# Six V transfers on GpSimd's DMA queue, and the fourth head's K issued in earlier slots, at the start of an attention and MLP kernel

## The chip, the cores and the metric

One core of one Trainium2 chip. The metric is the device time of the whole kernel in microseconds (us), from one launch; lower is better. Engines are named as the profile names them: PE (TensorE, matmuls), PEld (its weight loads), DVE (VectorE), ACT (ScalarE), POOL (GpSimd) and SP (SyncE, which here only issues DMAs).

## The reference

```python
x  = A_x                                # 1 x 2048 x 512, bf16
xn = _layernorm(x)
s  = _A_ref(xn, k_cache, v_cache, wq, wo)   # 32 heads of 128, 2048 queries, 2048 keys:
                                            # softmax(q k^T / sqrt(128)) v, then @ wo
g  = _silu(_B_ref(xn, w1, w2, w3, w4))      # a mixer with shifted channels, then an MLP
return x + s * g
```

K and V come from a cache in HBM (32 heads x 2048 x 128 each). Nearly all the work is the attention: for each head, 2048 x 2048 scores, their exponentials, and the product with V.

## The kernel before, in words

**Units and slots.** The 32 heads are taken in 8 groups of four. A unit is one head with 512 of the 2048 queries; inside a group the four heads follow each other for the first 512 queries, then for the next, so units 0 to 3 are heads 0 to 3 with the first 512 queries. A unit has 8 slots, and the main loop (line 809) runs over all slots n; unit u has slots 8u to 8u + 7. Each slot does one `s_slot` (L196): two score matmuls of 128 keys each into PSUM, and one exponential over both on ACT (L207). Five slots later (at this place of the program) the matching `pv_slot` (L225) multiplies the exponentials with two blocks of V. So the scores of unit u begin in slot 8u, and its product with V in slot 8u + 5. A quarter of K (512 keys) serves two slots: slot 8u needs the first quarter of its head's K, 8u + 2 the second, 8u + 4 the third and 8u + 6 the fourth. A half of V serves four slots of the product.

**The order.** Every instruction is pinned to the program's order on its engine (`pin`), so each engine and each DMA queue runs its list in exactly the order in which the Python code makes it; an instruction whose data isn't there holds up all behind it on its engine. Small pieces of work are hung on slots with `at(n, ...)` and are made at the end of slot n.

**What else runs in the first slots.** Tokens are normalized tile by tile: `ln1_load` fetches a tile of x on GpSimd's queue, `ln1_stats` takes the mean and variance on DVE and the inverse root on POOL (`rsqrt`, L126 and L127), `ln1_apply` normalizes on DVE (L423) and `ln1_turn` transposes by DMA on SP's queue (L439) into `xnT`. The query projection of later units (`q_mm`) reads `xnT`; that of unit 4 stands in slots 22 and 23 and is the first that needs token tiles 4 to 7. For the first four units the sums of the exponentials are made by a matmul with ones (`sums`, L235), inverted on DVE (L245, tile `rc`), written to DRAM on SP's queue (L247, `dr`), read back spread over all partitions on the same queue (L277, `rb`), and `norm` (L280, L294) multiplies the product with V by it on DVE. Unit u has its `dr` in slot 8u + 11, its `rb` in slot 8u + 12 and its `norm` in slot 8u + 18. The product lies in one of two PSUM tiles (`psO`), so that the product of unit u + 2, from slot 8u + 21 on, waits for the `norm` of unit u.

**The loads that the change touches.** `load_k` (L153) fetches a quarter of one head's K with a transposing DMA (L158); `load_v` (L162) fetches half of one head's V (L168). Both are issued on SP's queue. Before the loop (lines 740 to 756) all of head 0 and 1, and the first two quarters of head 2's K, are issued; the rest of heads 2 and 3 hang on slots 2 to 22 (lines 766 to 768). Later groups (lines 773 to 782) load in the same way from SP's queue, hung on their own slots; the change leaves them as they are. Each DMA also waits, before it is issued, until the eighth one ahead of it in its kind of queue has landed, since the DMAs share eight semaphores in turn.

Of the kernel before, what the change touches and what calls it, by code (L numbers as in the profile page):

```python
# [17 lines left out]
def kernel(  # L18
# [15 lines left out]
    nc = tc.nc  # L34
# [28 lines left out]
    pin = tc.keep_in_program_order  # L63
# [78 lines left out]
    def at(n, fn):  # L142
        todo[n].append(fn)
# [9 lines left out]
    def load_k(h, pieces):  # L153
        w = Sk // KSPLIT
        for i in pieces:
            if i == 0:
                kTs[h] = kp.tile([P, Sk], BF16, name="kT")
            pin(nc.sync.dma_start(  # L158
                out=kTs[h][:, i * w:(i + 1) * w],
                in_=A_k_cache[0, h, i * w:(i + 1) * w, :], transpose=True))  # L160

    def load_v(h, halves):  # L162
        v = A_v_cache[0, h].rearrange("(i p j) d -> p i j d", p=P, j=KJ)
        for i in halves:
            if i == 0:
                vBs[h] = vp.tile([P, KC, Dh], BF16, name="vb")
            ks = slice(i * KSPLIT // 2, (i + 1) * KSPLIT // 2)
            pin(nc.sync.dma_start(  # L168
                out=vBs[h].rearrange("p (i j) d -> p i j d", j=KJ)[:, ks], in_=v[:, ks]))

    def load_w(h, eng=nc.sync):
# [266 lines left out]
    def ln1_turn(t):  # L438
        pin(nc.sync.dma_start_transpose(out=xnT[:, :, t * P:(t + 1) * P], in_=xns.pop(t)[:]))  # L439
# [304 lines left out]
    for h in range(HG - 1):  # L744
        load_w(h, nc.gpsimd)
    load_k(0, range(KSPLIT))
    load_v(0, (0, 1))
    load_k(1, range(KSPLIT))
    warm_up(WARM)
    mean_3 = first_stats()  # L750
    load_w(HG - 1, nc.gpsimd)
    for t in range(4, 8):
        ln1_load(t, nc.gpsimd)
    first_tokens()
    load_v(1, (0, 1))
    load_k(2, (0, 1))
    tokens = ((2, 4, 5), (5, 9, 11), (8, 12, 13), (11, 14, 14),
              (21, 27, 27), (26, 31, 31), (34, 37, 37), (38, 41, 41),
              (39, 45, 45), (47, 53, 53), (55, 61, 61), (63, 69, 69))
    for t, (stats, apply, turn) in enumerate(tokens, 4):  # L760
# [2 lines left out]
        at(stats, lambda t=t: ln1_stats(t))  # L763
        at(apply, lambda t=t: ln1_apply(t))
        at(turn, lambda t=t: ln1_turn(t))
    for n, load, h, piece in ((2, load_k, 2, 2), (4, load_k, 2, 3), (7, load_v, 2, 0), (15, load_k, 3, 0), (15, load_v, 2, 1),
                              (19, load_k, 3, 1), (20, load_k, 3, 2), (20, load_v, 3, 0), (21, load_k, 3, 3), (22, load_v, 3, 1)):
        at(n, lambda load=load, h=h, piece=piece: load(h, (piece,)))
    at(28, ph1_load)
    at(64, w2_load)  # L770
    for h in range(HG):
# [1 line left out]
    for g in range(NG - 1):  # L773
        b = (g * QT + QT - 1) * HG
        for hh in range(HG):
            h = (g + 1) * HG + hh
# [163 lines left out]
    halves = [psX.tile([P, D], FP32, tag="xm", name="ps_wo"), psO.tile([P, D], FP32, tag="ps_o", name="ps_wo")]  # L940
# [51 lines left out]
```

## Time and profile before

| | |
|---|---|
| Time, median of 3 runs | 1250.77 us (1249.69 to 1251.74) |
| Profiled execution: span from its first to its last instruction | 1248.0 us |
| Profiled execution: time of its own | not shown beside its span; the median of the runs is 2.8 us above the span |
| PE busy | 1240.0 us (99%) |
| ACT busy | 1128.1 us (90%) |
| DVE busy | 1115.1 us (89%) |
| POOL busy | 134.8 us (11%) |
| DMA, mean over the span | 104 GB/s |

How to read it: busy times are sums over the span, and PE's are modelled, since matmuls are pipelined. A view of the timeline has, in each row, the start (us from the span's start), the duration, the engine, the line of the kernel, the operation, and the tiles written and read; in brackets stands how long the engine was idle before it and which instruction ended that. This is inferred from semaphores: where the engine named had long been done, it was another, often a DMA. An engine with a "q" (SPq) is the issuing of a DMA, not the transfer; from issue to landing has rows of its own. Tile names are the program's: `kT` and `vb` are K and V of a head, `pT` the exponentials, `ps_s` and `ps_o` the scores and the product with V in PSUM, `xin` a tile of x, `acc` the running sum of exponentials.

### The profile page before, as it was taken

How to read it: one execution, taken by the hardware profiler on the slowest of the kernel's cores; microseconds unless marked ns; L12 is line 12 of the kernel's file. 1: busy time of each engine (PE TensorE's matmuls, PEld its weight loads, DVE VectorE, ACT ScalarE, POOL GpSimd, SP SyncE). 2: the span in 40 equal slices, each digit the busy share in tenths (PEclk: the TensorE clock that was granted, in tenths of full speed). 3: DMA queues.
4: the chain of work that ended last, by engine and by line, in shares of the span. 5: the costliest groups of instructions: out<-in, count | busy, mean ns of one | idle time of the engine just before them, and what ended most of it. 6: DMA issues, size and time to landing. Idle time of an engine off the chain costs nothing.

```text
span 1248.0 us, 16489 instructions
## 1 busy us (share of the span) xinstructions
PE 1240.0 (99%) x5808; PEld 597.1 (48%) x5808; DVE 1115.1 (89%) x1518; ACT 1128.1 (90%) x1285; POOL 134.8 (11%) x237
## 2 busy tenths in 40 slices
PE   9999999999999999999999999999999999999998
PEld 5444444444444444444444444444444444444444
DVE  7899999999899988889998889999888999888997
ACT  8999999888999888899998889998888999988992
POOL 4310003332101000000100000010000000000110
PEclk9999999999999999999999999999999999999999
DMA  9654353565624456243563345734345243653453
GB/s 183 138 115 73 72 135 73 124 134 111 153 63 112 104 103 118 51 94 73 108 155 85 68 77 106 135 81 81 82 103 121 55 89 68 125 140 75 106 156 99
DMA packets 240468, 129.32 MB, mean 104 GB/s; under 512 B 191296, under 2 KB 217280, under 8 KB 240384
## 3 DMA queue, kind: packets, MB, share of 16 engines
q1 hardware_dynamic: 231136, 102.89, 41.0%
q0 software_dynamic: 8672, 24.91, 7.5%
q8 instruction: 45, 0.74, 0.3%
q10 hardware_dynamic: 576, 0.46, 0.1%
q14 instruction: 39, 0.32, 0.1%
HBM read 83.62 MB, written 8.13 MB: 74 GB/s over the span
## 4 chain that ended last, share of the span: by engine, by line
PE 98%; ACT 1%; DVE 0%; issue 0%; POOL 0%; POOLq 0%
PE ps_s L122 36%; PE ps_o L122 35%; PE ps_m L122 10%; PE ps_q L122 9%; PE ps_wo L122 8%; ACT pT L207 1%; DVE acc L218 0%; ACT sq L513 0%; ACT pre L540 0%; DVE xnT L469 0%; DVE qT L193 0%; ACT xnT L471 0%; PE ps_sum L122 0%; DVE gf L350 0%; DVE xf L355 0%
## 5 line engine op out<-in xcount | busy, mean ns | idle before, releaser
L207 ACT ACTIVATE pT<-ps_s 128x1024 bf16<-128x1024 f32 x1024 | 1022.1, 1028 | 92.3 <-PE ps_s L122 77.4
L122 PE MATMUL ps_s<-qT,kT 128*128 128x512 bf16 x2048 | 608.8, 379 | 1.3 <-ACT pT L207 0.9
L122 PE MATMUL ps_o<-pT,vb 128*128 128x512 bf16 x2048 | 607.5, 379 | 0.0
L122 PEld LDWEIGHTS <-kT 128*128 128x128 bf16 x2048 | 231.6, 113 | 228.4 <-issue 4.5
L218 DVE TENSOR_TENSOR acc<-acc,pT 128x2048 bf16<-128x2048 bf16 x256 | 308.9, 1207 | 8.9 <-ACT pT L207 8.4
L122 PEld LDWEIGHTS <-vb 128*128 128x128 bf16 x2048 | 200.2, 98 | 225.6
L213 DVE TENSOR_TENSOR acc<-pT 128x2048 bf16<-128x2048 bf16 x128 | 156.3, 1221 | 32.8 <-ACT pT L207 32.4
L122 PE MATMUL ps_q<-xnT,wq_h 128*128 128x512 bf16 (+1 forms) x524 | 152.8, 374 | 0.6 <-ACT xnT L471 0.4
L122 PE MATMUL ps_wo<-wo_h,oT 128*128 128x512 bf16 (+1 forms) x460 | 135.3, 377 | 0.5 <-DVE qT L193 0.5
L287 DVE TENSOR_TENSOR oT<-ps_o,rb 128x512 bf16<-128x512 f32 x122 | 130.7, 1072 | 4.4 <-DMA rb<-dr 4.1
L373 DVE TENSOR_TENSOR s_acc<-ps_wo,s_acc 128x512 f32<-128x512 f32 x96 | 66.0, 688 | 42.7 <-PE ps_wo L122 42.6
L222 DVE TENSOR_TENSOR acc<-acc 128x1024 bf16<-128x1024 bf16 x128 | 87.5, 684 | 0.9
L260 DVE TENSOR_REDUCE sm<-accT 128x4 f32<-128x512 bf16 x122 | 83.1, 681 | 1.5 <-DMA accT<-acc 1.4
L193 DVE CAST qT<-ps_q 128x512 bf16<-128x512 f32 x109 | 75.0, 688 | 8.4 <-PE ps_q L122 7.7
L122 PEld LDWEIGHTS <-wq_h 128*128 128x128 bf16 x524 | 50.8, 98 | 60.8 <-issue 1.0
L122 PE MATMUL ps_m<-xn2T,w_sb 128*128 128x512 bf16 x224 | 77.1, 379 | 0.0
L122 PE MATMUL ps_m<-w_sb,h2T 128*128 128x512 bf16 x224 | 77.1, 379 | 0.0
L122 PEld LDWEIGHTS <-oT 128*128 128x128 bf16 x468 | 45.7, 98 | 55.2 <-issue 0.8
L671 POOL DMA_DIRECT2D w_sb<-in_B_w_dram x28 | 21.1, 754 | 370.6 <-PE ps_m L122 370.6
L223 DVE TENSOR_TENSOR acc<-acc 128x512 bf16<-128x512 bf16 x128 | 54.4, 425 | 4.4
L699 POOL DMA_DIRECT2D g_d<-xr x16 | 8.7, 546 | 438.0 <-DVE xr L697 372.2
L508 DVE SCALAR_TENSOR_TENSOR sq<-sq,pre 128x1024 bf16<-128x1024 bf16 x36 | 44.0, 1222 | 4.6 <-ACT sq L504 4.6
(87 smaller groups left out, 591.0 us busy)
## 6 DMA issues: line engine op xcount, KB each, us to landing
rb<-dr SPq DMA_DIRECT2D x127, 256.0 KB, 4.0
vb<-in_A_v_cache_dram SPq DMA_DIRECT2D x64, 256.0 KB, 3.3
w_sb<-in_B_w_dram POOLq DMA_DIRECT2D x28, 256.0 KB, 3.6
wo_h<-in_A_wo_dram SPq DMA_DIRECT2D x32, 128.0 KB, 2.9
wq_h<-in_A_wq_dram SPq DMA_DIRECT2D x28, 128.0 KB, 2.9
kT<-in_A_k_cache_dram SPq DMA_TRANSPOSE x128, 3.4
dr<-rc SPq DMA_DIRECT2D x128, 2.0 KB, 1.7
xr<-in_A_x_dram POOLq DMA_DIRECT2D x16, 128.0 KB, 2.4
```

The lines of the kernel that those rows point to most:

```text
L122: pin(nc.tensor.matmul(out=out, lhsT=lhsT, rhs=rhs, start=start, stop=stop))
L193: pin(nc.vector.tensor_copy(out=qT[:], in_=st[u].pop("psq")[:]))
L207: pin(nc.scalar.activation(out=s["pT"][-1][:, jj:jj + 2, :], in_=sps[:], func=ACT.Exp, scale=SCALE))
L213: pin(nc.vector.tensor_tensor(out=s["acc"][:], in0=s["pT"][0][:], in1=s["pT"][1][:], op=ALU.add))
L218: pin(nc.vector.tensor_tensor(out=a[:], in0=a[:], in1=st[u]["pT"][i][:], op=ALU.add))
L222: pin(nc.vector.tensor_tensor(out=a[:, 0:2, :], in0=a[:, 0:2, :], in1=a[:, 2:4, :], op=ALU.add))
L223: pin(nc.vector.tensor_tensor(out=a[:, 0, :], in0=a[:, 0, :], in1=a[:, 1, :], op=ALU.add))
L260: pin(nc.vector.tensor_reduce(out=sm[:], in_=s.pop("at")[:], axis=mybir.AxisListType.X, op=ALU.add))
L287: pin(nc.vector.tensor_tensor(out=oTs[(g, qt)][:, hh, :].rearrange(f, j=4), in0=s["o"].rearrange(f, j=4), in1=s["rb"].rearrange("x (p j) - ...
L373: pin(nc.vector.tensor_tensor(out=sa, in0=ps[:], in1=sa, op=ALU.add))
L508: pin(nc.vector.scalar_tensor_tensor(out=sq[:].rearrange(f2), in0=sq[:].rearrange(f2), scalar=1.0, in1=pre[:].rearrange(f2), op0=ALU.add, ...
L671: pin(nc.gpsimd.dma_start(out=w[:], in_=w3_v[:, :, fc * P:(fc + 2) * P]))
```

## The change

```diff
-    def load_v(h, halves):
+    def load_v(h, halves, eng=nc.sync):
...
-            pin(nc.sync.dma_start(
+            pin(eng.dma_start(
                 out=vBs[h].rearrange("p (i j) d -> p i j d", j=KJ)[:, ks], in_=v[:, ks]))
...
-    load_v(1, (0, 1))
+    load_v(1, (0, 1), nc.gpsimd)
     load_k(2, (0, 1))
...
-    for n, load, h, piece in ((2, load_k, 2, 2), (4, load_k, 2, 3), (7, load_v, 2, 0), (15, load_k, 3, 0), (15, load_v, 2, 1),
-                              (19, load_k, 3, 1), (20, load_k, 3, 2), (20, load_v, 3, 0), (21, load_k, 3, 3), (22, load_v, 3, 1)):
-        at(n, lambda load=load, h=h, piece=piece: load(h, (piece,)))
+    for n, load, h, piece in ((2, load_k, 2, 2), (4, load_k, 2, 3), (7, load_v, 2, 0), (8, load_k, 3, 0), (9, load_k, 3, 1), (10, load_k, 3, 2), (15, load_v, 2, 1),
+                              (15, load_k, 3, 3), (20, load_v, 3, 0), (22, load_v, 3, 1)):
+        at(n, lambda load=load, h=h, piece=piece: load(h, (piece,), *([nc.gpsimd] if load is load_v else [])))
```

The V halves of the second, third and fourth head (`load_v` of 1, 2 and 3, six DMAs) go from SP's queue to GpSimd's, in the same slots. The four quarters of the fourth head's K (`load_k` of 3) stay on SP's queue and go from slots 15, 19, 20 and 21 to slots 8, 9, 10 and 15. In SP's list the first three of them now stand ahead of unit 0's `dr` and `rb` and of three token transposes; the fourth stands ahead of unit 1's `dr`. In GpSimd's list the second head's V stands behind the first four loads of x, the third head's halves behind the inverse roots of token tiles 5 and 7, and the fourth head's halves on either side of that of token tile 8. The lists of PE, DVE and ACT keep their instructions and their order.

## The prediction

> **What bounds the kernel now.** I read the shares of the chain of work first, then the busy time by stretch, then TensorE's timeline for the places where it stands still, and only then the queues behind those places.
>
> ```profile
> PE 98%; ACT 1%; DVE 0%; issue 0%; POOL 0%; POOLq 0%
> ```
> ```profile
> 30.00:60.00 30.00, 28.89 (x138) 13.65 (x137) 25.92 (x44) 27.18 (x30) 10.16 (x22) 1.00 0.71 150
> 100.00:1240.00 1140.00, 1140.00 (x5287) 545.50 (x5285) 1024.88 (x1372) 1038.00 (x1178) 104.86 (x175) 1.00 0.47 101
> ```
>
> The first line says that the chain that ended last is 98% TensorE. In the stretches (length, then busy time of PE, PEld, DVE, ACT and POOL, then the granted clock) PE is busy for 1140.00 of 1140.00 us behind 100 us, at clock 1.00: nothing that only touches loads can gain there. From 30 to 60 us it lacks 1.11 us. The order on PE is written out in the program and the edit leaves it alone, so a stall that goes shifts all that follows by its length, and a stall that comes does the same.
>
> TensorE's timeline (start, duration, line, tiles, idle before and who ended it) shows where:
>
> ```profile
> 20.08 0.59 PE L122 MATMUL ps_s<-qT,kT 128*128 128x512 bf16 x2
> ...
> 30.19 0.59 PE L122 MATMUL ps_s<-qT,kT 128*128 128x512 bf16 x2
> 30.62 0.59 PE L122 MATMUL ps_o<-pT,vb 128*128 128x512 bf16 x2
> ...
> 31.94 0.59 PE L122 MATMUL ps_q<-xnT,wq_h 128*128 128x512 bf16 x2
> ...
> 37.63 0.26 PE L122 MATMUL ps_sum<-ones_t,acc 128*128 128x1 bf16 x4
> 38.48 0.62 PE L122 MATMUL ps_s<-qT,kT 128*128 128x512 bf16 x2 [0.58 <-ACT pT L207]
> ...
> 54.93 0.59 PE L122 MATMUL ps_s<-qT,kT 128*128 128x512 bf16 x2
> 56.06 0.59 PE L122 MATMUL ps_wo<-wo_h,oT 128*128 128x512 bf16 x2 [0.53 <-DVE qT L193]
> ```
>
> Two stalls. A pair of matmuls that shows 0.59 is followed by the next after 0.43 (30.19 to 30.62), since their tails overlap, so each stall is worth some 0.15 us more than its idle: 54.93 + 0.43 = 55.36 against 56.06 is 0.70 us, and the first is likewise about 0.7. Counting the score pairs, 38.48 is slot 28, the fifth of the fourth head, which reads the third quarter of that head's K. The releaser printed (an exponential) is not the one: below is what SyncE does.
>
> ```profile
> 7.95 5.22 SPq L158 DMA_TRANSPOSE kT<-in_A_k_cache_dram  x4
> 13.22 1.09 SPq L168 DMA_DIRECT2D vb<-in_A_v_cache_dram  x2
> 14.36 6.15 SPq L158 DMA_TRANSPOSE kT<-in_A_k_cache_dram  x4
> 20.62 1.22 SPq L439 DMA_TRANSPOSE xnT<-xn  x1
> 21.89 0.58 SPq L168 DMA_DIRECT2D vb<-in_A_v_cache_dram  x1
> 22.91 0.34 SPq L247 DMA_DIRECT2D dr<-rc  x1
> 23.30 1.19 SPq L439 DMA_TRANSPOSE xnT<-xn  x1
> 25.27 0.34 SPq L277 DMA_DIRECT2D rb<-dr  x1
> 25.71 2.52 SPq L439 DMA_TRANSPOSE xnT<-xn  x2
> 28.28 1.27 SPq L158 DMA_TRANSPOSE kT<-in_A_k_cache_dram  x1
> ...
> 33.92 1.12 SPq L158 DMA_TRANSPOSE kT<-in_A_k_cache_dram  x1
> ```
> The issues taken one at a time, with the time from issue to landing: the K quarter of 33.92, the rb of 25.27, the dr of 22.91, the last xnT of the pair from 25.71, the third unit's dr (38.63), the fourth unit's dr (48.36); and the spread of all K quarters issued in the first 50 us:
> ```profile
> kT<-in_A_k_cache_dram SPq DMA_TRANSPOSE x1, 4.5
> rb<-dr SPq DMA_DIRECT2D x1, 256.0 KB, 4.1
> dr<-rc SPq DMA_DIRECT2D x1, 2.0 KB, 2.3
> xnT<-xn SPq DMA_TRANSPOSE x1, 4.3
> dr<-rc SPq DMA_DIRECT2D x1, 2.0 KB, 3.5
> dr<-rc SPq DMA_DIRECT2D x1, 2.0 KB, 1.5
> DMA to landing us min/median/max: 2.6/5.1/7.5
> ```
>
> The quarter issued at 33.92 landed 4.5 us later, at 38.4, and slot 28 starts at 38.48: the transfer released it. The second stall is VectorE's: it waits for a copy that VectorE reaches late, and VectorE's timeline shows why.
>
> ```profile
> 29.47 0.69 DVE L294 TENSOR_TENSOR oT<-ps_o,rb 128x512 bf16<-128x512 f32 x1 [0.58 <-PE ps_sum L122]
> ...
> 46.76 0.69 DVE L294 TENSOR_TENSOR oT<-ps_o,rb 128x512 bf16<-128x512 f32 x1 [1.02 <-DMA rb<-dr]
> ```
>
> It stood still 1.02 us for the third unit's rb, whose dr had taken 3.5 us behind two K and two V transfers of SyncE; the fourth unit's dr, with none before it, took 1.5. The row at 29.47 is the same thing once more, under a false name: 25.27 + 4.1 is 29.4.
>
> **The change part by part.**
>
> *Six V halves to GpSimd's queue.* Each takes 0.58 us off SyncE. On GpSimd they stand behind the row statistics of the tokens:
>
> ```profile
> 23.77 1.10 POOL L126 TENSOR_SCALAR ve<-mv 128x1 f32<-128x1 f32 x1 [0.25 <-DVE mv L397]
> ...
> 25.49 1.20 POOL L390 DMA_DIRECT2D xin<-in_A_x_dram  x2
> ```
>
> An issue there costs about 0.6 us (1.20 for two), POOL is idle most of this stretch (10.16 us of 30 busy), and no statistics pair has more than two V issues right ahead of it: cost nothing, hidden by that idle time. Uncovered, a late statistic would delay VectorE's normalization of one token tile by 0.6 us a V issue. The second head's V goes out about 3 us sooner and so shares the DMA engines with the second head's K. Its second quarter is read in slot 10, at 20.08; it is issued at about 9.3, and even the slowest K landing of the view, 7.5, is at 16.8. Cost taken: nothing, up to 3 us of delay.
>
> *Third head's K.* With 13.22 free of V, the four quarters run from 13.22 for 6.15 us, to 19.4; if the long issue among them (6.15 for four against 5.22) doesn't recur, to 18.4. The xnT behind them ends at 20.6 (19.7).
>
> *Fourth head's K.* Three quarters (slots 8 to 10) now come next: three times 1.30 (5.22 for four) is 3.9 us. They land before 30 us, the fourth is issued at about 29, and slot 28 has its data: **minus 0.7 us**. What is late next there: slot 29 and 30 need V's first half and K's last quarter, both now landed by 34.
>
> *What these three are moved past.* The first unit's dr stood at 22.91, just behind its data. It is now issued at 24.5 (23.5), 0.6 to 1.6 us later, and all behind it with it: xnT, rb, two xnT. The rb waits for the dr, which with K quarters ahead of it takes between the rows 1.5 and 3.5; I take 2.3, its own row in much the same company. So rb goes out 0.5 to 1.6 late, I take 0.9, and lands at 30.3 (29.4 before). Two things are due then. PE's row at 30.62 is slot 21, the first product with V of the third unit, into the PSUM tile that the first unit's normalization (29.47, 0.69 long) frees: it was free at 30.16, 0.46 ahead. And 31.94 needs the last xnT, which landed at 26.99 + 4.3 = 31.3, 0.65 ahead. With 0.9 us of delay the first makes a stall of 0.9 - 0.46 = 0.45, and this one covers the other (0.9 - 0.65 = 0.25). PE has no slack from there to 37.6. **Plus 0.45 us**; bounds: nothing, if the dr takes 1.5 and the K issues are short, and 2.1, if rb is 1.6 late and two V halves on the other queue (256 KB each, beside an rb of the same size) add another microsecond: 2.6 - 0.46.
>
> *The third unit's dr and rb.* Between 33.9 and 38 SyncE has now nothing to issue. I take the dr at 1.5 to 2 instead of 3.5, so the rb lands over 1.5 us sooner and VectorE's 1.02 of waiting goes. It then reaches the copy about 1.0 sooner, at or before PE wants it: **minus 0.7 us** (bounds: minus 0.3, if VectorE is still late by PE's own shift, and minus 0.85 with the gaps of 0.1 to 0.2 around it).
>
> *Behind 65 us* the queues hold the same transfers in the same order: nothing.
>
> **Sum:** -0.7 + 0.45 - 0.7 = -0.95 us. The profiled span is 1248.0; the runs' median 1250.77 lies 2.8 above it, which is what stands around the span and the spread of runs (1249.69 to 1251.74). With -0.95 the span would be 1247.1 and the median **1249.8**.
>
> **The rivals.**
>
> *No new stall.* The dr is so short and the K issues so even that rb lands by 29.9. For it: the 0.93 us of the long issue may not recur. Against: three K issues alone are 3.9 us, and the only gap that they can fill is V's 0.58 and 1.09. Time: -1.4, 1249.4.
>
> *The row of small transfers is late (ends slower).* Place: slot 21 and the q product at 31.94. Point: rb landing after 31.3, 1.4 us behind the free stall, eats both gains; then each microsecond costs one. Price: at the bound of 2.1, with the second gain down to 0.3, it is -0.7 + 2.1 - 0.3 = +1.1, 1251.9. For it: the dr rows of 3.5 behind K and V; DMA share 0.71 in that stretch. Against: POOL's V halves land in a time when SyncE's V are gone. The Trainium skill, page "DMA: Bandwidth & Descriptors", section "Queues, rings and completion order", says that each DMA engine takes a ring's descriptors in order, so that a small transfer doesn't overtake large ones of its own queue; by that rule the dr would be nearer 3.5 than 1.5 and the sum nearer this rival. The trace agrees in kind: 3.5 behind transfers, 1.5 without.
>
> *GpSimd's issues stretch (slower too).* VectorE is busy most of this time, and if its work holds GpSimd's issues, V comes late. The second half of the third head's V stands behind one x load at 25.5 and is read in slot 25, four slots behind 30.62, after 34.1 at the earliest. With a landing of 5.1 us (the median of the K view) it is late if each issue takes over 1.75 us, since 25.5 + 2 x 1.75 + 5.1 is 34.1; at 3 us it costs 2.5, which less both gains of 1.4 is +1.1, 1251.9; a second such wait, for the fourth head's V, would add another 2.5, 1254.4. Against: the two issues at 25.49, beside VectorE's adds, took 1.20 together, and the longest hold near them is the 1.10 of the one-element instruction. The Trainium skill, "SBUF — State Buffer", section "Who interferes with whom", speaks against the move: GpSimd cannot write its DMA descriptors while VectorE is in a two-port mode. The rows at 25.49 do not show it.
>
> *It doesn't do what it says.* ScalarE, not K, would hold slot 28: then the first gain is nothing and the second is made up for by the new stall, 1250.5. Against it: the landing at 38.4.
>
> **How the numbers follow.** Forecast (stall of 0.2 to 1.1 us) 0.45, 1249.8; no new stall 0.18, 1249.4; late small transfers 0.20, 1251.9; stretched GpSimd issues 0.11, 1251.9 to 1254.4; no effect 0.06, 1250.5. All but a part of the third and fourth lie within 0.2% (2.5 us) of before, which is about what a measurement of this kernel can tell from no change. Faster by more than that (under 1248.3) needs more than both stalls, and comes only from the spread of the runs: 0.07. Slower (over 1253.3): three quarters of the GpSimd case and a quarter of the late one, with the spread, 0.08 + 0.05 = 0.13. Same: 0.80. The range takes 1249.4 less the runs' 1.1 below and 1251.9 and 1.0 above: 1248.3 to 1252.9.
>
> **What would show it.** Slot 28 without idle time; K's third quarter landed before 30; the first dr issued at 23.5 to 24.6 and a stall of PE at slot 21 or at the first q product near 32; the third unit's dr below 2.5 us and no wait of VectorE near 46; no stall at 56. Wrong: a stall of PE over 2 us anywhere, a GpSimd V issue over 1.75 us, or PE's busy time behind 100 us below its length.

## The result, and the profile after

| | before | changed |
|---|---|---|
| Median of 6 runs each | 1250.89 us (1249.69 to 1253.04) | 1256.73 us (1252.99 to 1259.63) |
| Ratio | | 1.0044, 95% interval 1.0033 to 1.0055 |
| Median in a second comparison (29 and 12 runs) | 1251.39 us (1248.81 to 1253.89) | 1256.31 us (1251.17 to 1261.62) |
| Ratio in that one | | 1.0034, 95% interval 1.0019 to 1.0048 |
| Profiled execution: own time, span | span 1248.0 | 1257.13, span 1255.4 |

The change makes the kernel 0.34 to 0.44% slower, some 5 us. The forecast was 1 us faster. The runs of the changed kernel also scatter more, over 10 us in the second comparison against 5.

The chain of work of the changed kernel, and its busy time by stretch (length; busy time of PE, PEld, DVE, ACT and POOL; granted clock; DMA share; GB/s):

```profile
PE 94%; DMA 2%; DVE 2%; ACT 1%; SPq 1%; issue 0%; POOL 0%; DVEq 0%; POOLq 0%
```
```profile
30.00:60.00 30.00, 24.73 (x112) 11.28 (x111) 19.59 (x33) 22.32 (x24) 8.31 (x20) 0.94 0.52 118
60.00:100.00 40.00, 39.43 (x182) 18.61 (x182) 39.46 (x59) 37.83 (x47) 8.74 (x15) 1.00 0.53 114
100.00:1240.00 1140.00, 1139.42 (x5281) 545.05 (x5280) 1024.05 (x1367) 1045.45 (x1186) 104.28 (x175) 1.00 0.49 100
```

Before, PE lacked 1.11 us from 30 to 60 us; now it lacks 5.27, and its clock there is 0.94 in place of 1.00. Behind 60 us little is different (0.57 and 0.58 us missing, before 0.06 and nothing; the first holds the stall that stood at 56 us before and is now at 62.9). So nearly all of the 7.4 us of span were lost in one place, and the chain now has DMA and SyncE in it. TensorE's timeline there:

```profile
30.60 0.59 PE L122 MATMUL ps_s<-qT,kT 128*128 128x512 bf16 x2
36.38 0.96 PE L122 MATMUL ps_o<-pT,vb 128*128 128x512 bf16 x2 [5.19 <-DVE oT L294]
37.13 1.06 PE L122 MATMUL ps_s<-qT,kT 128*128 128x512 bf16 x2
...
45.05 0.27 PE L122 MATMUL ps_sum<-ones_t,acc 128*128 128x1 bf16 x4
45.19 0.60 PE L122 MATMUL ps_s<-qT,kT 128*128 128x512 bf16 x2
...
62.89 0.59 PE L122 MATMUL ps_wo<-wo_h,oT 128*128 128x512 bf16 x2 [0.53 <-DVE qT L193]
```

The stall at slot 28 is gone, as forecast: 45.19 follows the sums without idle time (38.48 had 0.58). The stall near 56 is still there, at 62.89, with the same 0.53. And at slot 21 (30.62 before) stands a new one of 5.19 us, more than ten times what was forecast. The matmul pairs behind it take 1.06 where those before it take 0.59; the stretches around it show why (same columns as above):

```profile
31.00:36.00 5.00, 0.19 (x1) 0.00 (x0) 0.36 (x1) 1.36 (x2) 0.00 (x0) 1.00 0.64 145
36.00:40.00 4.00, 3.62 (x9) 1.27 (x9) 3.42 (x6) 1.02 (x1) 1.47 (x2) 0.57 0.18 37
40.00:44.00 4.00, 4.00 (x20) 1.88 (x19) 2.64 (x4) 3.17 (x4) 0.94 (x2) 1.00 0.57 133
```

The granted clock was 0.57 over the 4 us behind the stall, which lost another (1 - 0.57) x 4 = 1.7 us. Against the kernel before, the rows add up so: the matmul of slot 21 starts 5.76 us later (36.38 against 30.62), the clock adds 1.66 by the sums (45.05 against 37.63), slot 28 gives 0.71 back (45.19 against 38.48), and some 0.7 of the 7.4 is left for all that comes later.

Who made PE wait: `norm` of the first unit, which waited for its rb. VectorE's row, SyncE's timeline, and from issue to landing the second quarter of the second head's K (issued at 10.12), the dr of 27.66 and the rb of 32.38:

```profile
35.64 0.69 DVE L294 TENSOR_TENSOR oT<-ps_o,rb 128x512 bf16<-128x512 f32 x1 [6.18 <-DMA rb<-dr]
```
```profile
7.97 14.34 SPq L158 DMA_TRANSPOSE kT<-in_A_k_cache_dram  x8
22.43 1.23 SPq L439 DMA_TRANSPOSE xnT<-xn  x1
23.70 3.87 SPq L158 DMA_TRANSPOSE kT<-in_A_k_cache_dram  x3
27.66 0.52 SPq L247 DMA_DIRECT2D dr<-rc  x1
28.23 1.22 SPq L439 DMA_TRANSPOSE xnT<-xn  x1
32.38 0.34 SPq L277 DMA_DIRECT2D rb<-dr  x1
```
```profile
kT<-in_A_k_cache_dram SPq DMA_TRANSPOSE x1, 9.9
dr<-rc SPq DMA_DIRECT2D x1, 2.0 KB, 4.6
rb<-dr SPq DMA_DIRECT2D x1, 256.0 KB, 3.2
```

Read from the end: rb landed at 35.55 (before 29.4), having gone out at 32.38 (before 25.27). It waited for the dr, which was issued at 27.66 (before 22.91) and took 4.6 us (before 2.3). The dr's issue stood behind the three K quarters, 3.87 us, and these behind the K of the second and third head, whose eight issues took 14.34 us, to 22.3, where the forecast had 19.4.

### The profile page after: what moved, and what is told of

Same layout as the page of the kernel before. It is cut to its first block, busy times and chain, and to the rows that moved or that the text cites. A ratio compares the mean times of both kernels' runs of the same rounds, so it can differ in the third digit from the quotient of the medians.

```text
span 1255.4 us, 16489 instructions
## 1 busy us (share of the span) xinstructions
PE 1242.1 (99%) x5808; PEld 596.9 (48%) x5808; DVE 1114.6 (89%) x1518; ACT 1129.1 (90%) x1285; POOL 138.6 (11%) x243
## 4 chain that ended last, share of the span: by engine, by line
PE 94%; DMA 2%; DVE 2%; ACT 1%; SPq 1%; issue 0%; POOL 0%; DVEq 0%; POOLq 0%
PE ps_s L122 34%; PE ps_o L122 33%; PE ps_m L122 10%; PE ps_wo L122 8%; PE ps_q L122 8%; DMA xin<-in_A_x_dram 1%; ACT pT L207 1%; DMA rb<-dr 1%; DMA dr<-rc 1%; DVE acc L218 0%; SPq L158 0%; DVE bn L396 0%; DMA kT<-in_A_k_cache_dram 0%; DVE oT L294 0%; DVE qT L193 0%
## 5 line engine op out<-in xcount | busy, mean ns | idle before, releaser
L122 PEld LDWEIGHTS <-oT 128*128 128x128 bf16 x468 | 45.7, 98 | 55.2 <-issue 0.8
```

What stands on the lines that cost most here:

```text
L122: pin(nc.tensor.matmul(out=out, lhsT=lhsT, rhs=rhs, start=start, stop=stop))
```

## The experiments

The theory after the result: unit 0's dr and rb, and the token transposes, are late because three K quarters stand ahead of them in SyncE's list (**order**), and V on GpSimd makes K's transposes and their issue slower (**V beside**). The rivals name one of the two alone, or chance. Each experiment below computes all of the reference, and each ratio is against runs of the kernel before on the same chip. It is worked out from all the runs, so it can differ by up to 0.07% from that of the two medians beside it. The rows and landings are of one profiled execution each, and one execution can differ from the next by microseconds.

**V part alone.** The fourth head's K back in slots 15, 19, 20 and 21:

```diff
-(8, load_k, 3, 0), (9, load_k, 3, 1), (10, load_k, 3, 2), ... (15, load_k, 3, 3)
+(15, load_k, 3, 0), (19, load_k, 3, 1), (20, load_k, 3, 2), ... (21, load_k, 3, 3)
```

> Only the V part of the change: six V halves on GpSimd's queue, the fourth head's K in its old slots 15, 19, 20, 21. Chain theory (three K quarters ahead of unit 0's dr make it late, V on GpSimd makes the third head's K issue slower): K of head 3 ends near 22.3 us as in the changed kernel, but dr goes out at about 23.7 and not 27.7, rb lands at 30 to 31, PE stalls 0.3 to 1.3 us at slot 21 and the clock does not fall; time 0 to 1 us above before. Rival (GpSimd's V alone does the harm): rb lands near 35 as in the changed kernel, stall over 4 us, 5 to 6 us above before.

1253.40 us against 1251.63, ratio 1.0009 (1.0001 to 1.0018). The profiled execution took 1252.37 us, the shortest of the eleven. The rb landed at 30.28 and slot 21 lost 0.30 us, as the theory had it; but 1 us later came a stall that neither had: the query projection waited 2.2 us for the last token transpose, issued at 27.11. Its waiting row, and the landing of that transpose:

```profile
PE ps_q L122 <- DMA xnT<-xn: 2.2, 1, 2.2
```
```profile
xnT<-xn SPq DMA_TRANSPOSE x1, 7.5
```

Before, the same transpose took 4.3 us. Two V halves of 256 KB each were on GpSimd's queue beside it. So V alone does harm, but not all of it, and in this execution on the transposes rather than on the dr. The move also changes when V comes: the fourth head's first half went out at 27.52 in place of 35.09, and from 25 to 35 us the DMA engines moved 1.63 MB at a share of 0.86, before 1.40 MB at 0.62. More bytes at that time, on whichever queue, is a rival that no run here separates from the second queue.

**K part alone.** All V on SyncE as before, K in slots 8, 9, 10 and 15:

```diff
-load_v(1, (0, 1), nc.gpsimd)
+load_v(1, (0, 1))
...
-load(h, (piece,), *([nc.gpsimd] if load is load_v else []))
+load(h, (piece,))
```

> Only the K part: fourth head's K in slots 8, 9, 10, 15, all V on SyncE's queue. Chain theory: K of head 3 ends near 20.5 as before, xnT and one V half follow, three K quarters end at about 26.3, dr out at 26.3 (before 22.9), landed by 29 to 30, rb landed at 33 to 34: PE stalls 3 to 4 us at slot 21, slot 28 does not stall, 2 to 4 us above before, more if the clock falls behind the stall. Rival (GpSimd's V alone does the harm): dr lands within 2.5 us, stall under 1 us, time at or below before.

1254.57 us against 1251.63, ratio 1.0019 (1.0010 to 1.0027). SyncE's timeline, and PE's wait (its releaser is printed as a token transpose; the product with V waits for `norm`, and that for the rb, which landed at 33.12):

```profile
22.18 0.58 SPq L168 DMA_DIRECT2D vb<-in_A_v_cache_dram  x1
22.81 3.75 SPq L158 DMA_TRANSPOSE kT<-in_A_k_cache_dram  x3
26.66 0.52 SPq L247 DMA_DIRECT2D dr<-rc  x1
27.23 1.21 SPq L439 DMA_TRANSPOSE xnT<-xn  x1
29.63 0.34 SPq L277 DMA_DIRECT2D rb<-dr  x1
```
```profile
33.96 0.92 PE L122 MATMUL ps_o<-pT,vb 128*128 128x512 bf16 x2 [3.21 <-DMA xnT<-xn]
```

3.21 us at slot 21, the clock halved behind it, and 2.9 us above before, as the theory had it. Without any V on GpSimd the K quarters alone put the dr 3.75 us back. The rival that blames GpSimd's V alone falls.

**The second head's V back on SyncE**, the other four halves on GpSimd, K early:

```diff
-load_v(1, (0, 1), nc.gpsimd)
+load_v(1, (0, 1))
```

> The changed kernel with the second head's V alone back on SyncE's queue ahead of the third head's K; the other four V halves stay on GpSimd. Chain theory: without 512 KB of V beside them on the other queue the K quarters of heads 2 and 3 land as before (5 to 7 us instead of 8 to 10), no K issue takes 4 us, the third head's K ends near 20.5, dr goes out at about 25.7 and rb lands at 31.5 to 34: stall 1.5 to 4 us, 1 to 4 us above before and 2 to 4 below the changed kernel. Rival (V on GpSimd costs nothing, the three K quarters do all): same time as the changed kernel.

1256.78 us against 1251.63, ratio 1.0034 (1.0023 to 1.0045): the same as the changed kernel, though no K issue took 4 us. The dr went out at 26.57, the rb landed at 33.62 and slot 21 lost 3.42 us. The theory's 2 to 4 us of gain did not come, so by the times the second head's V is not what costs. The profile splits the loss otherwise: a shorter stall than the changed kernel's 5.19, but the clock halved for twice as long, 6.8 us.

**K behind the chain.** All V on GpSimd, all four quarters of K in slot 15:

```diff
-(8, load_k, 3, 0), (9, load_k, 3, 1), (10, load_k, 3, 2), ... (15, load_k, 3, 3)
+(15, load_k, 3, 0), (15, load_k, 3, 1), (15, load_k, 3, 2), (15, load_k, 3, 3)
```

> All six V halves on GpSimd; the fourth head's K all four in slot 15, so behind unit 0's dr and rb and the token transposes, ahead of unit 1's dr. Chain theory: dr out at about 23.7, rb landed at 30 to 31, stall 0.3 to 1.3 us at slot 21; no stall at slot 28 (K's third quarter issued by 33, landed by 37), clock full: between 1 us below and 1 us above before. Rival (GpSimd's V alone does the harm): as the changed kernel, 5 to 6 us above before.

1254.70 us against 1251.63, ratio 1.0019 (1.0009 to 1.0029): 3 us above before, between the two theories. The profiled execution took 1258.12 us, the longest of the twelve. In it the second head's K landed so late (20.83 for its second quarter) that slot 10 stalled for 0.8 us, the rb landed at 33.31, and the two stalls for `norm` took 3.6 us together. But up to slot 15 its lists are those of the V part alone, so a difference ahead of that is not the edit's. SyncE's rows there, then here:

```profile
7.95 13.33 SPq L158 DMA_TRANSPOSE kT<-in_A_k_cache_dram  x8
23.02 0.34 SPq L247 DMA_DIRECT2D dr<-rc  x1
```
```profile
7.95 15.29 SPq L158 DMA_TRANSPOSE kT<-in_A_k_cache_dram  x8
24.68 0.52 SPq L247 DMA_DIRECT2D dr<-rc  x1
```

The same list put the dr at 23.02 in one execution and at 24.68 in the other, and the rb's landing at 30.28 and 33.31. With all V on GpSimd the delay can be there even when the K quarters stand behind the dr, but not in each execution. The last token transpose took 4.3 us here, beside the same two V halves on GpSimd.

**One quarter of K, nothing else.** On the kernel before:

```diff
-(19, load_k, 3, 1), (20, load_k, 3, 2),
+(19, load_k, 3, 1), (19, load_k, 3, 2),
```

> The kernel before with one edit: the third quarter of the fourth head's K from slot 20 to slot 19, so that SyncE issues it while unit 1's dr is on its way and not behind unit 1's rb. Theory (of the kernel before, only the stall at slot 28 is K's, and it goes when that one quarter is issued before 33 us, with nothing put ahead of unit 0's dr): issued at about 32, landed by 36.5, no stall at slot 28; 0.3 to 1.4 us below before. Rival (any K moved ahead of a dr or rb costs as much as it gains): unit 1's rb later by over 1 us and VectorE waits for it; at before or above.

1251.44 us against 1251.44, ratio 0.9993 (0.9982 to 1.0003): no measurable difference. But the trace shows the step at work:

```profile
37.49 0.27 PE L122 MATMUL ps_sum<-ones_t,acc 128*128 128x1 bf16 x4
37.62 0.60 PE L122 MATMUL ps_s<-qT,kT 128*128 128x512 bf16 x2
```

No stall at slot 28. In that execution stalls of 0.2 to 0.7 us came at 40 and 43.5 instead, behind a rb that landed at 38.51 (37.00 before): the rival's mechanism, about as large as the gain.

**Unit 0's dr and rb off SyncE's list.** The changed kernel, with

```diff
-pin(nc.sync.dma_start(out=s["dr"][:], in_=rc[:]))
+pin((nc.gpsimd if s is st.get(0) else nc.sync).dma_start(out=s["dr"][:], in_=rc[:]))
...
-pin(nc.sync.dma_start(
+pin((nc.gpsimd if u == 0 else nc.sync).dma_start(
     out=st[u]["rb"][:], ...
```

> The changed kernel, with unit 0's dr and rb issued on GpSimd's queue in place of SyncE's. Order theory (they were late because they stood behind the three K quarters in SyncE's list): dr out at about 24 and landed by 27, rb landed at 30 to 31.5, stall at slot 21 under 1.5 us in place of 5.2; the token transposes still stand behind the K quarters, so a stall of 1 to 3 us comes at the q product one slot later; clock full or halved for a short time; 2 to 5 us below the changed kernel. Rival (the DMA engines were full, the place in the list matters little): rb lands at 34 or later, stall over 4 us, time as the changed kernel.

1256.52 us against 1251.44, ratio 1.0035 (1.0021 to 1.0048). GpSimd's timeline, PE's waits, then V's landing and the last token transpose's, and the two queues' packets, MB and share of 16 engines from 26 to 38 us:

```profile
23.06 0.63 POOL L247 DMA_DIRECT2D dr<-rc  x1
...
25.73 0.63 POOL L277 DMA_DIRECT2D rb<-dr  x1 [0.61 <-DMA dr<-rc]
```
```profile
PE ps_q L122 <- DMA xnT<-xn: 4.8, 1, 4.8
PE ps_o L122 <- DVE oT L294: 1.0, 1, 1.0
```
```profile
vb<-in_A_v_cache_dram POOLq DMA_DIRECT2D x1, 256.0 KB, 9.1
xnT<-xn SPq DMA_TRANSPOSE x1, 9.4
```
```profile
q0 software_dynamic: 401, 1.31, 64.9%
q1 hardware_dynamic: 2727, 0.62, 45.7%
```

The order part is shown here: off the list the dr goes out at 23.06, before the last of the three K quarters (24.16), rb at 25.73, and the stall at slot 21 falls to 1.0 from 5.2 (2.7 in a second profile of the changed kernel, below). The Trainium skill, page "DMA: Bandwidth & Descriptors", section "Queues, rings and completion order", has each DMA engine take the descriptors of one ring in order. The traces agree: in all thirteen the transfers on SyncE's queue landed in the order of their issue. The landing of the dr alone doesn't show it, though: 2.4 us here, 4.6 and 2.0 behind the three K quarters. And the time stays, as the rival had it: the token transposes, on SyncE beside 1.31 MB on GpSimd's queue (V, loads of x, and now the rb), took up to 9.4 us, and the stall moved one slot on, to the query projection, 4.8 us. What was expected as 1 to 3 us there was larger, and the gain of 2 to 5 us did not come.

**The second head's V alone on GpSimd**, on the kernel before:

```diff
-load_v(1, (0, 1))
+load_v(1, (0, 1), nc.gpsimd)
```

> The kernel before with only the second head's V halves on GpSimd's queue (the third and fourth head's V on SyncE's as before). Theory (this V beside the second head's K is what makes K land in 8 to 10 us and one K issue take 4 us, and the third and fourth head's V on GpSimd are what made the token transposes late when V alone was moved): one K issue near 15 us of 3.5 to 4.3 us, second head's K quarters landing in 8 to 10 us, dr at 23 to 23.7, last token transpose landed by 32.5, no stall over 1 us at slots 21 and 22; within 1 us of before. Rival (the second head's V is the whole harm of the V part): 1 us or more above before, with a stall of 2 us at slot 22.

1252.30 us against 1251.44, ratio 1.0001 (0.9988 to 1.0013): nothing. K's issue of 3.26 us came, K took 6 to 9 us, the last transpose landed at 30.91, and slots 21 and 22 did not stall; the third head's K has the slack for it. Slot 28 stalled for 1.2 us, 0.6 more than before. The profiles point to the third and fourth head's halves for the harm of the V part; the times (1.0009 and 1.0001, each to about 0.1%) can't tell the two apart.

**The fourth head's V alone on GpSimd**, with the last two K quarters a slot earlier, on the kernel before:

```diff
-(20, load_k, 3, 2), (20, load_v, 3, 0), (21, load_k, 3, 3), (22, load_v, 3, 1)
+(19, load_k, 3, 2), (20, load_k, 3, 3), (22, load_v, 3, 0), (22, load_v, 3, 1)
...
-load(h, (piece,))
+load(h, (piece,), *([nc.gpsimd] if load is load_v and h == 3 else []))
```

> The kernel before with the third quarter of the fourth head's K in slot 19, the fourth in slot 20, and the fourth head's two V halves on GpSimd's queue in slot 22, behind token tile 8's statistics. Theory (unit 2's dr takes 3.5 us because two K and two V transfers stand ahead of it in SyncE's list; GpSimd's queue does no harm where no token transpose is on its way): no stall at slot 28, unit 2's dr lands in 2.5 us or less, no wait of VectorE for its rb, stall near 56 us below 0.4; 0.5 to 1.8 us below before. Rival (V on GpSimd lands late beside the rest): V's first half lands after 40, a stall at slot 29, above before.

1250.56 us against 1251.44, ratio 0.9989 (0.9978 to 0.9999): the fastest of all, if only by 0.1%, with an interval that ends just short of none; among eleven comparisons that can be chance. No stall at slot 28, and the stall at 56 fell to 0.4, but VectorE still waited 0.8 us for unit 2's rb, and V's first half took 6.1 us and slot 29 waited for it:

```profile
39.81 0.61 PE L122 MATMUL ps_o<-pT,vb 128*128 128x512 bf16 x2 [0.74 <-DMA vb<-in_A_v_cache_dram]
```

**The changed kernel once more.**

> The changed kernel unaltered, beside the two below. Theory (the stall at slot 21 comes with the list orders and not by chance): 4 to 6.5 us above before, PE stall at slot 21 of 3.5 us or more, clock near 0.5 for 2 to 5 us behind it. Rival (the profiled execution was an unlucky one): stall under 2 us in this profile.

1256.31 us against 1251.39, ratio 1.0034 (1.0019 to 1.0048). This profiled execution was a quick one: span 1249.5, dr out at 25.10 and landed in 2.0 us, rb landed at 32.27, the stall at slot 21 only 2.7 us, and the clock behind it full:

```profile
33.11 0.59 PE L122 MATMUL ps_o<-pT,vb 128*128 128x512 bf16 x2 [2.68 <-DVE oT L294]
```
```profile
35.00:37.00 2.00, 2.00 (x10) 0.91 (x9) 1.86 (x4) 1.40 (x3) 1.75 (x3) 1.00 0.20 54
```

So the stall came in both executions seen, at 2.7 and 5.2. Neither theory's number for it was met (3.5 or more; under 2); the time was as the theory had it, 4.9 us above before.

**V on ScalarE's queue instead.** The V part alone, two of the halves on ScalarE's hardware queue:

```diff
+nc.scalar if (h, piece) in ((2, 1), (3, 0)) else nc.gpsimd
```

> As the kernel with the V part only, but the third head's second V half and the fourth head's first (slots 15 and 20) on ScalarE's hardware queue. Theory (GpSimd's queue moves in packets of some 3 KB against 0.25 KB of SyncE's transposes, so each turn it gets costs the transposes most of the engines): V's packets on ScalarE's queue are smaller, the last token transpose lands in 5 us or less instead of 7.5, stall at slot 22 under 1 us. Rival (any second queue slows the transposes): landing in 6 to 8 us, stall of 2 us or more at slot 22. ScalarE's exponentials lose about 0.5 us for each of the two issues, so the time itself is worth little here.

1251.74 us against 1251.39, ratio 1.0008 (0.9994 to 1.0022). The last token transpose landed in 5.4 us, between the theory's 5 and the rival's 6 to 8, and slot 22 lost 0.3. Inconclusive: ScalarE reached the second of the two issues only at 29.8, when the transposes were nearly through (on GpSimd it was 27.5). Later, at slot 28, K waited 2.0 us beside the last V half on GpSimd.

**One V half on GpSimd**, the fourth head's second, with V's first half on SyncE again. Against the run with the fourth head's V alone on GpSimd (cut to the slots):

```diff
-(20, load_k, 3, 3), (22, load_v, 3, 0), (22, load_v, 3, 1)
+(20, load_v, 3, 0), (20, load_k, 3, 3), (22, load_v, 3, 1)
```

> The kernel before with the third and fourth quarter of the fourth head's K in slots 19 and 20, its first V half on SyncE in slot 20 as before, and only its second V half on GpSimd's queue. Theory: no stall at slot 28, none over 0.3 us at slot 29 (V's first half landed by 38.5), unit 2's dr in 2.6 us or less; 0.7 to 1.9 us below before, ratio 0.9985 to 0.9995. Rival (the gaps only move): a stall of 0.5 us or more at slots 29 to 33, ratio 0.9995 or above.

1250.97 us against 1251.39, ratio 1.0003 (0.9994 to 1.0012): the rival's case. The stall at slot 28 went, and one came at slot 30, 2.6 us, for the fourth quarter of K, which took 8.5 us beside one V half of 8.4:

```profile
PE ps_s L122 <- DMA kT<-in_A_k_cache_dram: 2.6, 1, 2.6
```

**What follows together.** K part alone +0.19%; V part alone +0.09%, with nothing measurable from the second head's V by itself; both +0.34 to +0.44%. Order is shown (K alone makes the stall, and moving dr and rb off the list cuts it to 1.0). That transposes on SyncE land later when V is on GpSimd's queue beside them was seen in some executions (7.5, 9.4 and 8.5 us against 4.3 and 3.9) and not, or hardly, in others (the last token transpose took 4.3 us with K behind the chain and 5.0 in the second profile of the changed kernel). Whether the second queue does it, or V's earlier time, and what happens inside the DMA engines, is not shown. The packets of GpSimd's queue are large (1.31 MB in 401, against 0.62 MB in 2727). The Trainium skill, page "DMA: Bandwidth & Descriptors", section "Queues, rings and completion order", has an engine change between rows packet by packet, by which large packets would take most of the time. That fits (64.9% against 45.7% in the view above) and is only argued: the one run that changed the packet size, with V on ScalarE's queue (0.52 MB in 544 packets from 26 to 38 us), was inconclusive.

## Why the prediction was wrong, point by point

**What bounds the kernel: right.** Two stalls, at slot 28 and near 56 us, one made by the third K quarter. Every run that issued it earlier lost the first stall.

**The fourth head's K: right.** Three quarters in 3.9 us (3.87 measured), slot 28 without idle time.

**What they are moved past: the step that failed, in size.** The prediction had the place (slot 21, through dr, rb and `norm`) and put it at "Plus 0.45 us", bounds nothing to 2.1, from an rb 0.9 us late. Measured: stalls of 5.2 and 2.7 in the changed kernel, 3.2 with the K part alone, from an rb that landed 6.2, 2.9 and 3.7 us late, of which only 0.46 was free. Three terms were too small, each in some of these profiles.

- *The issue of the dr.* 22.91 + 1.6 was worked out from the row of 6.15 as it stood, but 0.9 was taken, on the chance that the long K issue would not recur. It recurred, longer (4.2, 2.8 and 2.3 us for one issue in these three profiles), and the dr went out 4.8, 2.2 and 3.8 us late.
- *Its landing.* 2.3 was taken; 4.6, 2.0 and 3.0 came. A nearer row had been at hand: the second unit's dr at 30.28, right behind one K and one V issue, took 3.2 (issued at 30.28, landed at 33.51). The rows of 3.5 and 1.5 were also read too simply: of the two K ahead of the first, one had landed at 38.43, and ahead of the second a token transpose and a load of `wo_h` were still on their way, until 48.73 and 49.26.
- *The landing of the rb.* 4.1 was taken as before, and a microsecond more only in the bound. In the second profile of the changed kernel, where the dr landed in 2.0, the rb took 5.1, and this made 1.0 of the 2.9 us.

**The V halves on GpSimd: "cost nothing" failed.** The issues themselves did as forecast. GpSimd's timeline in the changed kernel:

```profile
26.06 0.63 POOL L390 DMA_DIRECT2D xin<-in_A_x_dram  x1
26.69 0.73 POOL L168 DMA_DIRECT2D vb<-in_A_v_cache_dram  x1
27.40 0.59 POOL L390 DMA_DIRECT2D xin<-in_A_x_dram  x1
27.98 0.71 POOL L168 DMA_DIRECT2D vb<-in_A_v_cache_dram  x1
```

What was not costed is the other side: what V, sooner and on a second queue, does to the transposes that SyncE has on the way. "The slowest K landing of the view, 7.5" was taken for a bound; it was a figure of K without V beside it, and 9.9 came. By itself the V part made the kernel 0.09% slower.

**The third unit's dr and rb: failed.** The dr did land sooner, but in 2.5 us in place of 3.5, where 1.5 to 2 was taken, although no other transfer was on its way when it went out at 45.81. The rb took 5.2 in place of 4.6 and VectorE still waited 1.2 us for it, so the 0.53 us at `ps_wo` stayed and the minus 0.7 did not come. Why the rb took longer is not shown: loads of x and of `w_sb` stand beside it both before and after.

**No term for the clock.** A stall was priced at its own length. Those of 3.2 us and more, and one of 2.6, cost more: 1.7 us in the profiled execution of the changed kernel. Its other runs probably lost more. In 4 of the first 6 and 6 of the second 12 the mean granted clock was 0.997, as in the two profiles in which the clock was halved for 6.8 us (the second head's V back on SyncE, dr and rb on GpSimd); the profiled runs showed 0.999 and 1.000.

**The rivals.** "The row of small transfers is late" was the right mechanism at the right place, with a chance of 0.20 and a price of +1.1 where +5 came. "GpSimd's issues stretch" did not happen: 0.71 to 0.78 us each, beside VectorE's adds and one normalization. The Trainium skill's rule ("SBUF — State Buffer", "Who interferes with whom") that GpSimd's descriptors wait for VectorE's two-port modes shows in none of these rows. "It doesn't do what it says" was wrong: slot 28 was K's.

## What to carry to other kernels

Where a small transfer sits in a chain that frees a PSUM tile (dr, rb, `norm`, the next product), find out how many microseconds it may be late, and count every issue moved ahead of it at its full length, with its landing too; here the slack was 0.46 us and one K quarter takes 1.26. A load that is late by 0.7 us is better brought forward by one place in the list than by ten slots, though here even one place gained nothing measurable (ratio 0.9993). A second DMA queue takes issue time off the first, but it also brings its transfers forward, and the first one's transposes beside them can land several microseconds later (7.5 in place of 4.3 us here), so look what is in flight at that time.

## What the runs showed of the hardware that was not expected

- **TensorE's clock falls at a stall.** Idle times of 2.0, 2.2, 2.7 and 2.7 us (V on ScalarE's queue, V part alone, K behind the chain, the second profile of the changed kernel) left it at 1.00. Those of 3.2 (K part alone), 3.4 (the second head's V back), 4.8 (dr and rb on GpSimd) and 5.2 us (the changed kernel) halved it, and so did one of 2.6 (one V half on GpSimd), so idle length alone does not settle it. It stayed halved for 3.4 us with the idle times of 2.6, 3.2 and 5.2, and for 6.8 us with those of 3.4 and 4.8. Stretches of the run with dr and rb on GpSimd, whose stall ended at 37.53, then of the one with the second head's V back, whose stall went from 31.04 to 34.46:

```profile
37.00:40.00 3.00, 2.46 (x6) 0.86 (x6) 0.00 (x0) 0.56 (x1) 0.00 (x0) 0.50 0.37 106
40.00:43.00 3.00, 3.00 (x8) 1.06 (x7) 1.82 (x2) 1.40 (x2) 0.00 (x0) 0.50 0.29 70
```
```profile
33.00:34.00 1.00, 0.00 (x0) 0.00 (x0) 0.29 (x1) 0.00 (x0) 0.00 (x0) 0.62 1.21 266
34.00:40.00 6.00, 5.32 (x13) 1.91 (x14) 3.50 (x6) 2.05 (x2) 2.42 (x3) 0.50 0.36 74
```

  The 0.62 of the third line is full clock for 0.24 us and half for the rest: the clock fell at about 33.24, 2.2 us into the stall. The Trainium skill, "TensorE: Matmul & The Clock Gate", Part 1, gives half rate after an idle window of about 3.4 us, watched by a free-running window. The 0.50 and the lengths of 3.4 and twice 3.4 agree, and a window that runs freely would explain 2.6 and 2.7 on either side; but 2.6 and 3.2 us of idle time, and 2.2 so far, were enough here, so by these rows a window need not be idle from end to end.
- **One K transpose's issue can take 4 us** (eight issues in 14.34 us, where eight at 1.30 would be 10.4) when much is on the way: the longest issue was 2.2 us in the kernel before, 2.3 with the K part alone, and 2.8 to 4.2 with the second head's V on GpSimd's queue. What it waits for is not shown.
- **The kernel before scatters by itself**: 1248.8 to 1257.7 us over some 100 runs. The intervals above reach about 0.1% to either side, so that is about the least that these comparisons show.
